# A feed-forward block with all 28 column tiles in pairs of seven products, and ten first products run ahead

## The chip, the cores and the metric

The kernel runs on one core of one Trainium2 chip. The metric is the device time of one execution in microseconds (us).

Short names: PE is the tensor engine (PEld its weight loads), DVE the vector engine, ACT the scalar engine, POOL the GpSimd engine, SP the engine that issues most of the loads.

## The reference

```python
B, S, D, F = 32, 32, 1024, 3584          # 1024 rows of x, bf16
def reference(x, w_gate, w_up, w_down):
    return (_gelu(x @ w_gate) * (x @ w_up)) @ w_down
```

## The kernel before

The hidden width of 3584 is 28 column tiles of 128. x is cut into two halves of 512 rows (`x0`, `x1`). Two column tiles, a left and a right one, together with the two halves of the rows and of the inner dimension, make a 2x2 block product. It needs 8 block products directly, and 7 in the Winograd form used here. A block product of one weight (gate or up) is four matmuls of 128x128 by 128x512, so for the two weights a pair costs 7 x 2 x 4 = 56 matmuls, where two tiles done directly cost 64.

Products 1 and 2 use plain bf16 operands. Products 3 to 7 use sums (and two plain operands) kept as fp32r: `S` holds the sums of x, `T` those of the weights.

Thirteen pairs cover 26 tiles. Tiles 0 and 1 are done directly. For four pairs product 1 runs ahead, at the start, when only `x0` is there: product 2 follows it into the same bank, which gives the left tile's first half of rows, and a copy of product 1 is kept for later. Such a pair is called short.

```python
LEFT = [2, 3] + list(range(4, 14)) + [14]
RIGHT = [26, 27] + list(range(16, 26)) + [15]
NP, EARLY = len(LEFT), 4
... (tiles 0 to 3 with x0: 64 matmuls, tiles 0 and 1 with x1: 32 matmuls)
for p in (2, 3):                                  # run ahead: products 1 and 2
    at = 25.8 + (p - 2) * 3.46
    g, u = 2 * p, 2 * p + 1
    for b, j, k0 in ((g, 0, 0), (u, 1, 0), (g, 0, 4), (u, 1, 4)):
        for k in range(k0, k0 + 4):
            mm(b, stat(p, j, k), x0[:, k, :], k == 0, k in (3, 7), add=k > 3)
        if k0 == 0:
            act(kept[p][:, j, :], bank(b), COPY, at + 0.9 * (j + 1))
    ...
sums_x(0, 21) ... sums_w(0, 4, 33.9)              # what the first pair needs
for p in range(NP):
    short, last = p < EARLY, p == NP - 1
    ...
    if short:
        for j in range(2):
            act(bank(B[j]), kept[p][:, j, :], COPY, at(0.1 + j * 0.1))
    else:
        for j in range(2):
            product(1, j, A[j], True)
            move(A[j], B[j], at(0.95 * (j + 1)))
    product(5, 0, E[0], True)
    ... (6, 7, 3 and 4; a full pair ends with product 2)
    sums_w(p + 1, 0, at(o + 1), "pool", [t4])     # T of the next pair: POOL, DVE, ACT
```

An `at` is only a sorting key: engines other than PE execute their instructions in that order, PE in the order of the program. Waits come from tracked reads and writes. After the pairs comes the down projection, 392 matmuls, which the change leaves alone but for the engine of its last copies.

## Time and profile before

| what | value | where it is read |
|---|---|---|
| time | 275.11 us (274.6 to 275.31) | three executions |
| span | 272.7 us, clock 1.00 | profile page |
| PE busy | 98% of the span | profile page |
| bf16 matmul to bf16 matmul | 0.216 us | starts of PE |
| fp32r matmul to fp32r matmul | 0.227 us | starts of PE |
| full pair, short pair | 12.56 us, 9.07 us | timelines of PE and DVE |

The head of the profile page of the kernel before: busy microseconds of each engine with its share of the span and its instructions, then busy tenths in 40 equal slices.

```profile
PE 268.1 (98%) x1186; PEld 188.1 (69%) x1200; DVE 189.2 (69%) x221; ACT 125.7 (46%) x195; POOL 45.4 (17%) x27
PE   8999999999999999999999999999999999999995
PEclk9999999999999999999999999999999999999999
PE 98%; issue 0%; DVE 0%
```

The last line is the chain of waits that ended last, by engine: followed back from the end it hardly leaves PE. The timeline of PE in the kernel before (start us, length us, what, count; a missing record here and there lowers a count by one):

```profile
4.61 28.16 PE L117 MATMUL ps<-arena 128*128 128x512 bf16 x126
32.42 36.66 PE L117 MATMUL ps<-S,T 128*128 128x512 f32 x160
...
92.54 3.40 PE L117 MATMUL ps<-arena 128*128 128x512 bf16 x15
95.59 9.44 PE L117 MATMUL ps<-S,T 128*128 128x512 f32 x40
105.10 3.40 PE L117 MATMUL ps<-arena 128*128 128x512 bf16 x15
...
182.24 24.12 PE L117 MATMUL ps<-arena,hT 128*128 128x512 bf16 x109
```

Up to 32.42 us PE works on bf16 products that need no sums. Then four short pairs follow in one piece (160 = 4 x 40 matmuls), then nine full pairs of 105.10 - 92.54 = 12.56 us each, and at 182.24 us the down projection starts.

### The profile page before, as it was taken

To read this page: it belongs to the slowest core of one execution; us is meant where nothing else is said; L and a number is where in the kernel's file an instruction comes from. 1 tells how busy PE (TensorE), PEld (TensorE's weight loads), DVE (VectorE), ACT (ScalarE), POOL (GpSimd) and SP (SyncE) were. 2 spreads that over 40 slices of the span, in tenths; PEclk is the share of its full clock that TensorE was granted. 3 is DMA by queue.
4 is the path that set the end of the run, shared out by engine and by line. 5 is a ranking of instruction groups with operands and counts; after the bars stand their busy time and mean duration, and the time that the engine had idled before them with its cause. 6 is when DMAs were issued, how large, how long until landed. Compare 5 with 4: busy or idle time off the path is not lost.

```text
span 272.7 us, 3266 instructions
## 1 busy us (share of the span) xinstructions
PE 268.1 (98%) x1186; PEld 188.1 (69%) x1200; DVE 189.2 (69%) x221; ACT 125.7 (46%) x195; POOL 45.4 (17%) x27
## 2 busy tenths in 40 slices
PE   8999999999999999999999999999999999999995
PEld 4444588888767686868676776664447888888884
DVE  1059978988583939374664739289962999999942
ACT  2344757566556474646455564521220112255561
POOL 1000032035326060524335160000000000000000
PEclk9999999999999999999999999999999999999999
DMA  7999412954700090047005000995011000001112
GB/s 184 270 207 300 117 39 60 281 202 124 186 0 0 21 286 2 0 129 179 1 4 154 0 2 0 302 350 159 0 38 38 2 0 0 1 2 58 38 58 77
DMA packets 44783, 26.42 MB, mean 97 GB/s; under 512 B 8416, under 2 KB 44768, under 8 KB 44768
## 3 DMA queue, kind: packets, MB, share of 16 engines
q1 hardware_dynamic: 42544, 24.25, 32.3%
q10 hardware_dynamic: 2224, 1.97, 2.8%
q8 instruction: 9, 0.15, 0.2%
q14 instruction: 6, 0.05, 0.1%
HBM read 22.28 MB, written 2.10 MB: 89 GB/s over the span
## 4 chain that ended last, share of the span: by engine, by line
PE 98%; issue 0%; DVE 0%
PE ps L117 98%; DVE arena L117 0%
## 5 line engine op out<-in xcount | busy, mean ns | idle before, releaser
L117 PE MATMUL ps<-S,T 128*128 128x512 f32 x520 | 122.0, 393 | 0.0
L117 PEld LDWEIGHTS ps<-S,T 128*128 128x128 f32 x520 | 97.7, 188 | 21.3
L117 ACT ACTIVATE tmp<-ps 128x512 f32<-128x512 f32 x64 | 38.1, 598 | 62.0 <-PE ps L117 62.0
L117 POOL TENSOR_TENSOR T<-arena 128x1024 fp32r<-128x1024 bf16 x21 | 44.7, 2149 | 117.1 <-PE ps L117 66.7
L117 PE MATMUL ps<-arena 128*128 128x512 bf16 x261 | 59.0, 379 | 0.8
L117 PE MATMUL ps<-T,S 128*128 128x512 f32 x224 | 51.3, 390 | 0.0
L117 ACT ACTIVATE ps<-ps 128x512 f32<-128x512 f32 x52 | 30.2, 583 | 42.0 <-PE ps L117 42.0
L117 DVE TENSOR_TENSOR hT<-tmp,ps 128x512 bf16<-128x512 f32 x56 | 37.2, 684 | 17.3 <-PE ps L117 14.9
L117 DVE TENSOR_TENSOR T<-arena,T 128x1024 fp32r<-128x1024 bf16 x40 | 48.4, 1217 | 0.1
L117 PEld LDWEIGHTS ps<-arena 128*128 128x128 bf16 x272 | 25.1, 98 | 33.4 <-issue 3.4
L117 PEld LDWEIGHTS ps<-T,S 128*128 128x128 f32 x224 | 42.1, 188 | 8.8
L117 DVE TENSOR_TENSOR tmp<-ps,tmp 128x512 f32<-128x512 f32 x26 | 18.0, 692 | 41.9 <-PE ps L117 41.9
L117 DVE TENSOR_TENSOR T<-arena 128x1024 fp32r<-128x1024 bf16 x19 | 22.7, 1218 | 7.4 <-PE ps L117 7.4
L117 PE MATMUL ps<-arena,hT 128*128 128x512 bf16 x109 | 24.0, 379 | 0.2
L117 DVE TENSOR_TENSOR ps<-ps,tmp 128x512 f32<-128x512 f32 x30 | 20.9, 695 | 2.8 <-PE ps L117 2.8
L117 PEld LDWEIGHTS ps<-arena,hT 128*128 128x128 bf16 x112 | 10.9, 98 | 13.2 <-issue 0.3
L117 ACT ACTIVATE tmp<-tmp 128x512 f32<-128x512 f32 x26 | 16.4, 632 | 4.2 <-DVE tmp L117 3.5
L117 DVE TENSOR_TENSOR S<-hT 128x1024 fp32r<-128x1024 bf16 x14 | 16.6, 1218 | 0.0
L117 ACT ACTIVATE T<-arena 128x1024 fp32r<-128x1024 bf16 x13 | 13.7, 1055 | 0.0
L117 PE MATMUL ps<-S 128*128 128x512 f32 x56 | 12.9, 389 | 0.0
L117 PEld LDWEIGHTS ps<-S 128*128 128x128 f32 x56 | 10.5, 188 | 2.2
L117 ACT ACTIVATE S<-arena 128x1024 fp32r<-128x1024 bf16 x9 | 9.4, 1057 | 4.3 <-PE ps L117 3.0
(25 smaller groups left out, 62.1 us busy)
## 6 DMA issues: line engine op xcount, KB each, us to landing
arena<-in_w_down_dram SPq DMA_DIRECT2D x4, 1792.0 KB, 10.5
arena<-in_w_gate_dram SPq DMA_DIRECT2D x11, 512.0 KB, 5.5
arena<-in_w_up_dram SPq DMA_DIRECT2D x11, 512.0 KB, 6.4
out_dram<-arena SPq DMA_DIRECT2D x12, 128.0 KB, 1.7
arena<-in_w_up_dram ACTq DMA_DIRECT2D x4, 128.0 KB, 4.5
arena<-in_w_gate_dram ACTq DMA_DIRECT2D x2, 256.0 KB, 5.0
arena<-in_w_up_dram ACTq DMA_DIRECT2D x2, 256.0 KB, 5.5
arena<-in_w_gate_dram SPq DMA_DIRECT2D x2, 256.0 KB, 6.3
```

Source lines behind the costliest of these rows:

```text
L117: ins = name(eng, *args, **kw) if callable(name) else getattr(eng, name)(*args, **kw)
```

## The change

Tiles 0 and 1 join the pairs: 14 pairs of tiles p and p + 14. The direct products of tiles 0 and 1 with the second half of x disappear, and PE would then run out of work before `x1` and its sums are ready. So products 1 and 2 of ten pairs instead of four run ahead. That needs the left weights of ten pairs early. There is no room for those of pairs 8 and 9, so they are put into half of the temporary buffer `tmp`, which the main loop overwrites, and are loaded a second time for the sums. The second pair of right weights takes the place of `x1` and is loaded once that has been read. The second half of x is now loaded after the weights of pairs 4 to 7. The first 64 matmuls now give eight copies of first products to keep instead of four; four of the eight are made by DVE, where all were made by ACT. The last output copies swap engines.

```diff
-        LEFT = [2, 3] + list(range(4, 14)) + [14]
-        RIGHT = [26, 27] + list(range(16, 26)) + [15]
-        NP, EARLY = len(LEFT), 4
+        NP, EARLY = 14, 10
+        kept = [piece(hT[:, m:m + 2, :]) for m in (14, 16, 18, 20, 22, 24, 26, 10, 12)] + [piece(o11[:, :, :])]
-        t0 = 33.0
+        t0 = 39.6
-        (tiles 0 and 1 with x1: 32 matmuls)
+        PLACE = [(None, 4096), (None, 0), (8192, 4096), (12288, 0), (20480, 24576), (8192, 12288), (20480, 24576)]
+        brief = tmp[:, 4:8, :] ...                    # pairs 8 and 9, while they run ahead
+        load_duo(2, 0, 10, None, 2, [begin_late])
+        load_duo(3, 0, 11, None, 2)
+        for k0 in range(0, DK, 2):
+            pr.add("sp", "dma_start_transpose", xT[1][:, k0:k0 + 2, :], xf[512:1024, ...], at=12, ...)
+        load_duo(4, 0, 13, brief)
+        load_duo(0, 1, 14)
-        for p in (2, 3):
-            at = 25.8 + (p - 2) * 3.46
+        for p in range(4, EARLY):
+            at = 18.9 + (p - 4) * 3.46
+            g = (0, 2, 4, 6, 2, 0)[p - 4]
+            for q, g, s in ((1, 2, 1), (3, 3, 1), (3, 4, 0), (3, 4, 1), (5, 5, 0), (7, 5, 1), (9, 6, 0), (9, 6, 1)):
+                if p == q:
+                    load_duo(g, s, t0)
             ... (cut: order of the first sums, names, the down projection's last copies)
```

More of the change, by code (lines that the diff above doesn't have):

```diff
@@ L161, in bass_standalone__geglu_ffn__sampling_kernel, with duo @@
         xT = [arena[:, a:a + 4096].rearrange("p (k n) -> p k n", n=512) for a in (16384, 0)]
-        raw_at = (20480, 8192)
-        raw = [arena[:, a:a + 8192].rearrange("p (s j k c) -> p s j k c", s=2, j=2, k=DK) for a in raw_at]
-        first = arena[:, raw_at[0]:raw_at[0] + 8192].rearrange("p (j k c) -> p j k c", j=2, k=DK)
-        near = arena[:, 4096:8192].rearrange("p (j k c) -> p j k c", j=2, k=DK)
+        first = arena[:, 20480:28672].rearrange("p (j k c) -> p j k c", j=2, k=DK)
+        def duo(a): return arena[:, a:a + 4096].rearrange("p (j k c) -> p j k c", j=2, k=DK)
         wd = [[arena[:, a:a + 7168].rearrange("p (k n) -> p k n", n=512) for a in row] for row in ((0, 7168), (14336, 21504))]
@@ L229, in bass_standalone__geglu_ffn__sampling_kernel, with piece @@
                 pr.add("dve", "tensor_copy", xT[0][:, k, i * 256:(i + 1) * 256], half)
-        LEFT = [2, 3] + list(range(4, 14)) + [14]
-        RIGHT = [26, 27] + list(range(16, 26)) + [15]
-        NP, EARLY = len(LEFT), 4
-        def left(p): return LEFT[p]
-        def right(p): return RIGHT[p]
-        kept = [hT[:, m:m + 2, :].rearrange("p t n -> p (t n)").bitcast(FP32).rearrange("p (j n) -> p j n", j=2)
-                for m in (10, 12, 22, 24)]
+        NP, EARLY = 14, 10
+        def piece(a): return a.rearrange("p t n -> p (t n)").bitcast(FP32).rearrange("p (j n) -> p j n", j=2)
+        kept = [piece(hT[:, m:m + 2, :]) for m in (14, 16, 18, 20, 22, 24, 26, 10, 12)] + [piece(o11[:, :, :])]
         SLOT = 0.9064
-        t0 = 33.0
+        t0 = 39.6
         T0 = []
@@ L257, in bass_standalone__geglu_ffn__sampling_kernel @@
             steps += [(m, j, k) for j in range(2) for k in range(DK - KO, DK)] + [(m, None, None)]
-        tile = lambda m: (m + 2) % 4
         for m, j, k in steps:
@@ L262, in bass_standalone__geglu_ffn__sampling_kernel @@
                 act(tmp[:, m, :], bank(2 * m), GELU, at)
-                tt(hT[:, tile(m), 0:512], tmp[:, m, :], bank(2 * m + 1), MUL, at)
+                tt(hT[:, m, 0:512], tmp[:, m, :], bank(2 * m + 1), MUL, at)
                 continue
-            op = mm(2 * m + j, first[:, j, k, tile(m) * P:(tile(m) + 1) * P], xT[0][:, k, :], k == 0, k in (3, DK - 1), add=k > 3)
-            if k == 3 and m < 2:
-                act(kept[m][:, j, :], bank(2 * m + j), COPY, 10.5)
+            op = mm(2 * m + j, first[:, j, k, m * P:(m + 1) * P], xT[0][:, k, :], k == 0, k in (3, DK - 1), add=k > 3)
+            if k == 3:
+                if m % 2 == 0:
+                    act(kept[m][:, j, :], bank(2 * m + j), COPY, 10.5)
+                else:
+                    pr.add("dve", "tensor_copy", kept[m][:, j, :], bank(2 * m + j), at=10.5)
             if (m, j) == (3, 1):
@@ L272, in bass_standalone__geglu_ffn__sampling_kernel, with load_duo @@
                 if k == 3:
-                    for k0 in range(0, DK, 2):
-                        load_x(1, k0, k0 + 2, [op])
-        steps = [(m, j, k) for m in range(2) for j in range(2) for k in range(KO)]
-        steps += [(m, j, k) for k in range(KO, DK - KO) for j in range(2) for m in range(2)]
-        for m in range(2):
-            steps += [(m, j, k) for j in range(2) for k in range(DK - KO, DK)] + [(m, None, None)]
-        for m, j, k in steps:
-            if j is None:
-                at = 25.0 + m * 0.87
-                act(tmp[:, m, :], bank(2 * m), GELU, at)
-                tt(hT[:, m, 512:1024], tmp[:, m, :], bank(2 * m + 1), MUL, at)
-                continue
-            mm(2 * m + j, first[:, j, k, m * P:(m + 1) * P], xT[1][:, k, :], k == 0, k == DK - 1)
-        def load_near(at):
-            for j in range(2):
-                dma("sp", near[:, j, :, :], w_r[j][:, :, right(0) * P:(right(1) + 1) * P], at, f"near{j}")
-        def load_pairs(gi, s, at, ks=slice(0, DK)):
-            for j in range(2):
-                m = (left, right)[s](2 * gi)
-                dma("sp", raw[gi % 2][:, s, j, ks, :], w_r[j][:, ks, m * P:(m + 2) * P], at, f"w{gi}_{j}{s}_{ks.start}")
-        load_near(10)
-        load_pairs(1, 0, 11, slice(0, 4))
-        load_pairs(1, 0, 11, slice(4, 8))
-        load_pairs(1, 1, 12)
+                    begin_late = op
+        PLACE = [(None, 4096), (None, 0), (8192, 4096), (12288, 0), (20480, 24576), (8192, 12288), (20480, 24576)]
+        brief = tmp[:, 4:8, :].rearrange("p t n -> p (t n)").bitcast(BF16).rearrange("p (j k c) -> p j k c", j=2, k=DK)
+        def load_duo(g, s, at, place=None, parts=1, after=()):
+            m, n = 2 * g + 14 * s, DK // parts
+            place = duo(PLACE[g][s]) if place is None else place
+            for k in range(0, DK, n):
+                for j in range(2):
+                    dma("sp", place[:, j, k:k + n, :], w_r[j][:, k:k + n, m * P:(m + 2) * P], at, f"w{g}{s}{j}{k}", after)
+                    after = ()
+        load_duo(2, 0, 10, None, 2, [begin_late])
+        load_duo(3, 0, 11, None, 2)
+        for k0 in range(0, DK, 2):
+            pr.add("sp", "dma_start_transpose", xT[1][:, k0:k0 + 2, :], xf[512:1024, k0 * P:(k0 + 2) * P], at=12, dma=f"x{k0}_1")
+        load_duo(4, 0, 13, brief)
+        load_duo(0, 1, 14)
         def load_wd(i, j, at):
@@ L307, in pair_w @@
         def pair_w(p, s, ks):
-            col = slice((p % 2) * P, (p % 2 + 1) * P)
-            if p < 2:
-                return first[:, :, ks, slice((p + 2) * P, (p + 3) * P)] if s == 0 else near[:, :, ks, col]
-            if p == NP - 1:
-                return raw[0][:, 0, :, ks, slice(s * P, (s + 1) * P)]
-            return raw[(p // 2) % 2][:, s, :, ks, col]
+            a = PLACE[p // 2][s]
+            if a is None:
+                return first[:, :, ks, p * P:(p + 1) * P]
+            return duo(a)[:, :, ks, (p % 2) * P:(p % 2 + 1) * P]
         def sx(s, k): return S[:, 4 * s + k:4 * s + k + 2, :]
@@ L327, in sums_x @@
                 elif s == 3:
-                    tt(sx(3, k), x0[:, k + 4:k + 6, :], sxf(1, k), SUB, at)
+                    tt(sx(3, k), x0[:, k + 4:k + 6, :], sxf(1, k), SUB, at + 1.5 * k)
                 else:
-                    act(sx(4, k), x1[:, k + 4:k + 6, :], COPY, at)
+                    act(sx(4, k), x1[:, k + 4:k + 6, :], COPY, at + 1.73 * k)
         def unit(p, u): return (5 * p + u) % 8
@@ L346, in sums_w, with stat @@
                 return tt(o, blk(1, 0), f(1), SUB, at, eng, after)
-        def stat(p, j, k): return pair_w(p, 0, slice(k, k + 1))[:, j, 0, :]
-        for p in (2, 3):
-            at = 25.8 + (p - 2) * 3.46
-            g, u = 2 * p, 2 * p + 1
+        def stat(p, j, k):
+            if p in (8, 9):
+                return brief[:, j, k, (p % 2) * P:(p % 2 + 1) * P]
+            return pair_w(p, 0, slice(k, k + 1))[:, j, 0, :]
+        for p in range(4, EARLY):
+            at = 18.9 + (p - 4) * 3.46
+            g = (0, 2, 4, 6, 2, 0)[p - 4]
+            u = g + 1
             for b, j, k0 in ((g, 0, 0), (u, 1, 0), (g, 0, 4), (u, 1, 4)):
@@ L357, in bass_standalone__geglu_ffn__sampling_kernel @@
                     act(kept[p][:, j, :], bank(b), COPY, at + 0.9 * (j + 1))
-            act(tmp[:, p, :], bank(g), GELU, at + 2.7)
-            tt(hT[:, left(p), 0:512], tmp[:, p, :], bank(u), MUL, at + 3.6)
-        sums_x(0, 21)
-        sums_x(1, 23.4)
-        sums_w(0, 0, 24.5)
-        sums_w(0, 1, 27)
-        sums_x(2, 28)
-        sums_w(0, 2, 29)
-        sums_x(3, 30.3)
-        sums_x(4, 22)
-        sums_w(0, 3, 28.6)
-        t4 = sums_w(0, 4, 33.9)
+            act(tmp[:, p % 4, :], bank(g), GELU, at + 2.7)
+            tt(hT[:, p, 0:512], tmp[:, p % 4, :], bank(u), MUL, at + 3.6)
+        sums_x(0, 27)
+        sums_x(1, 28)
+        sums_x(2, 30.5)
+        sums_w(0, 0, 33.5)
+        sums_w(0, 1, 34.5)
+        sums_w(0, 2, 36.5)
+        sums_x(3, 37.2)
+        sums_x(4, 28)
+        sums_w(0, 3, 36)
+        t4 = sums_w(0, 4, 40.5)
+        load_duo(1, 1, 34)
         B, C = (4, 5), (6, 7)
@@ L376, in bass_standalone__geglu_ffn__sampling_kernel @@
             A, E = ((0, 1), (2, 3)) if short or (p - EARLY) % 2 == 0 else ((2, 3), (0, 1))
-            if p % 2 == 0 and 2 <= p // 2 + 1 < (NP + 1) // 2:
-                load_pairs(p // 2 + 1, 0, t0)
-                if p < NP - 3:
-                    load_pairs(p // 2 + 1, 1, t0)
-            if p == 3:
+            for q, g, s in ((1, 2, 1), (3, 3, 1), (3, 4, 0), (3, 4, 1), (5, 5, 0), (7, 5, 1), (9, 6, 0), (9, 6, 1)):
+                if p == q:
+                    load_duo(g, s, t0)
+            if p == 7:
                 load_wd(0, 0, t0)
-            if last:
+            if p == 12:
                 load_wd(0, 1, t0)
-            ml, mr = left(p), right(p)
+            ml, mr = p, p + 14
             at = lambda s: t0 + s * SLOT
@@ L563, in done4 @@
         def done4(t, at):
-            if t % 2:
+            if t % 2 == 0:
                 pr.add("dve", "tensor_copy", late[:, 2, t, :], bank(PA[t]), at=at)
```

## The prediction

> **What bounds the kernel.** The tensor engine. The profile page gives PE 98% busy of a 272.7 us span, and the chain of waits that ended last is 98% PE, with pieces of "issue" of 0.05 to 0.07 us between; the granted clock is 1.00 in every slice. The Trainium skill ("Perfetto Trace Analysis", Identifying the Most-Contended Engine) warns that busy matmuls alone do not prove this, so I read rates from starts in the timeline of PE: bf16 products follow each other every 0.216 to 0.217 us (the first 128 from 4.61 to 32.42 us). A full pair takes 12.56 us (92.54 to 105.10), a short pair, whose first product was run ahead, 9.07 us (the same DVE step at 46.45, 55.52, 64.59). The waits view gives PE 0.8 us of idle in all, before the kernel's own work. So time follows the number and kind of matmuls, unless the change makes a gap.
>
> **Removed and added.** Before: 128 bf16 matmuls up front (tiles 0 and 1 done directly, 64 matmuls, first products of four pairs), then 4 short and 9 full pairs. After: 160 up front (first and second products of ten pairs), 10 short and 4 full pairs. The instruction order confirms 1184 matmuls become 1176: 48 fewer bf16, 40 more fp32r. From trace durations:
> - 32 more bf16 up front: 32 x 0.2173 = +6.95 us
> - 6 more short pairs: 6 x 9.07 = +54.42 us
> - 5 fewer full pairs: -62.80 us
> Sum -1.43 us, all on the critical path as PE is the chain. The last copy of an output tile goes from DVE (0.69 us) to ACT (0.60): perhaps -0.1 us more at the end.
>
> **Moved, expected free.** DVE does 8.5 us of work in each 9.07 us short pair (windows view: 8.9 of 10 us at 40:50 and 50:60) and made no PE gap there; ten such pairs instead of four repeat a steady state. Two loads of 1 MB are repeated, one of them at the start: the queue must now bring 5 MB behind the first x and weights instead of 4 MB. Packets of weights ran at about 285 KB per us until 30.2 us before, so about 33 us now. The risk lies here: the second half of x now comes after 2 MB of weights, so it lands near 28 instead of 21.2 us, and DVE then does eight sums of x (1.22 us each), three of weights and four products between 28 and 44 us. My hand schedule has the sums of the first pair ready 1 to 2.5 us before PE asks (first at 39.3 us). The weights of pair 4 must land by 18.4 us; I expect the first at 16.5 us.
>
> **Prediction.** 275.1 - 1.4 = 273.7 us; range 273.0 to 274.8. Faster by over 2%: 0.01; within 2%: 0.97; slower: 0.02.
>
> **What shows each step right or wrong.** Fp32r matmuls start near 39.3 us with no gap before; short pairs stay at 9.07 us through pair 9; PE waits stay near zero; the down projection begins near 180.8 us (before 182.24); after it nothing changes. If the second half of x comes late, PE has gaps between 39 and 46 us, released by DVE sums. If weights come late, PE weight loads wait for DMA at 18 to 33 us.
>
> **What would make it wrong.** A start-up stall by DMA order (up to 1 to 2 us, which would eat the gain); DVE falling behind over ten short pairs (its spare is only 0.5 us in each); weight loads for the later pairs arriving late because a buffer comes free only when the pair before it is done; copies of eight first products at 10.5 us, which have to clear a bank within 1.7 us.

## The result and the profile after

The first six executions of the changed kernel gave 273.31 us in the median, the fast ones from 272.91 to 273.66 us. One took 978.18 us, and it was the profiled one. It is treated apart at the end of this section. Run again (experiment 1) the changed kernel gave 273.55 us against 275.27 us, a ratio of 0.9941 with a 95% interval of 0.992 to 0.9961. A ratio here is the mean time of one kernel's fast runs over that of the other's of the same rounds, so it is not quite the ratio of the medians. The gain is real and well under 2%.

All readings of the changed kernel are from that second, fast profile. The head of its page, with the same lines as before, except that this trace has no record of the granted clock and so no PEclk line; that PE ran at full speed is read from its starts, which lie 0.216 and 0.227 us apart as before:

```profile
PE 266.3 (98%) x1182; PEld 190.6 (70%) x1192; DVE 203.1 (75%) x237; ACT 131.8 (49%) x210; POOL 37.1 (14%) x23
PE   8999999999999999999999999999999999999995
PE 98%; issue 0%; ACT 0%; DVE 0%
```

The timeline of PE in the changed kernel:

```profile
4.47 27.94 PE L117 MATMUL ps<-arena 128*128 128x512 bf16 x126 [0.34 <-DVE arena L117]
32.24 7.07 PE L117 MATMUL ps<-arena,tmp 128*128 128x512 bf16 x31
38.96 91.07 PE L117 MATMUL ps<-S,T 128*128 128x512 f32 x400
130.10 1.67 PE L117 MATMUL ps<-arena 128*128 128x512 bf16 x7
...
180.38 24.12 PE L117 MATMUL ps<-arena,hT 128*128 128x512 bf16 x109
```

The products of pairs 8 and 9, whose weights lie among the temporaries, are the second line. Ten short pairs (400 matmuls) run from 38.96 us without a gap; the down projection starts at 180.38 us. Between the two profiles the pair stage went from 182.24 - 32.42 = 149.82 us to 180.38 - 38.96 = 141.42 us, that is -8.40 us where the sum in the prediction says 54.42 - 62.80 = -8.38 us. The front went from 32.42 to 38.96 us, +6.54 us where the prediction says +6.95. The difference of 0.41 us is mostly the start-up, which varies from one execution to the next: counted from the event of the next paragraph the front grew by 6.92 us. After the pairs the two differ by -0.12 us, most of it the last copy.

**A yardstick free of the start-up.** ACT's first GELU of a product waits for the 50th of the first 64 matmuls. Its start ranges from 15.46 to 17.05 us in nine profiles, although those kernels issue the same PE work up to there. In the kernel before and in the changed one:

```profile
15.84 0.60 ACT L117 ACTIVATE tmp<-ps 128x512 f32<-128x512 f32 x1 [3.33 <-PE ps L117]
15.46 0.60 ACT L117 ACTIVATE tmp<-ps 128x512 f32<-128x512 f32 x1 [3.33 <-PE ps L117]
```

Two things make up the spread of 1.6 us, which is as much as the whole gain. One is the clock: in two of the starts (eight ahead, x first) matmuls still follow each other every 0.427 us, double the usual 0.216, until 6.3 and 6.5 us. The Trainium skill, "TensorE: Matmul & The Clock Gate", Part 1, says that PE starts at half clock, that the warm-up window runs freely, and that its cost varies from run to run. The traces agree: the first matmuls lie 0.427 us apart in all nine, and the last at half clock comes between about 3.4 and 6.5 us. The other is the first loads: with nine ahead PE was at full clock by then but lost 1.1 us waiting for x, and with eight ahead 0.6 us waiting for up weights. So in the table below the last column subtracts the whole start-up: span minus the start of the first GELU.

| kernel | median us | ratio to before, 95% | span - first GELU, us | against the changed kernel |
|---|---|---|---|---|
| before | 275.27 | 1 | 272.74 - 15.84 = 256.90 | +1.60 |
| changed | 273.55 | 0.992 to 0.9961 | 270.76 - 15.46 = 255.30 | 0 |
| loads twice | 273.59 | 0.992 to 0.9954 | 271.13 - 15.87 = 255.26 | -0.04 |
| sum on DVE | 273.07 | 0.9901 to 0.9956 | 271.08 - 15.81 = 255.27 | -0.03 |
| eight matmuls more | 275.17 | 0.9973 to 1.0004 | 273.39 - 16.36 = 257.03 | +1.73 |
| nine ahead | 274.98 | 0.9955 to 0.9998 | 273.63 - 16.72 = 256.91 | +1.61 |
| x later | 275.46 | 0.9981 to 1.0014 | 273.16 - 16.27 = 256.89 | +1.59 |
| x first | 277.62 | 1.0063 to 1.0124 | 274.54 - 16.71 = 257.83 | +2.53 |
| eight ahead | 278.86 | 1.0101 to 1.0141 | 277.33 - 17.05 = 260.28 | +4.98 |

The medians and ratios come from three sets of rounds on three chips, in which the kernel before had medians of 275.27, 275.40 and 275.23 us; each ratio is to the kernel before of the same rounds. The last two columns are of one execution each. The three kernels with no extra PE work or wait agree there within 0.04 us, while their medians spread over 0.5 us.

**The slow execution.** Its page has no line of the granted clock and its clock is given as 1.0; the fast profile of the changed kernel lacks that line too. The timeline of PE shows what happened:

```profile
35.38 40.54 PE L117 MATMUL ps<-arena 128*128 128x512 bf16 x49 [0.52 <-issue]
```

With one missing record these are 50 matmuls in 76.44 - 35.38 = 41.06 us, 0.82 us each against 0.216, from the start to the end. PE ran at about a quarter of its speed; nothing else was slow (the DVE sums took 1.22 us as always). The same kernel did not show it in its eleven other executions, and none of the variants did. It says nothing about the change, and it is left out of all comparisons.

### The profile page after: what moved, and what is told of

It is laid out like the page before. It is cut to its first block, busy times and chain, and to the rows that moved or that the text cites. A ratio compares the mean times of both kernels' runs of the same rounds, so it can differ in the third digit from the quotient of the medians.

```text
span 976.1 us, 3280 instructions
## 1 busy us (share of the span) xinstructions
PE 966.8 (99%) x1182; PEld 436.0 (45%) x1192; DVE 208.5 (21%) x237; ACT 134.8 (14%) x210; POOL 36.6 (4%) x23
## 3 DMA queue, kind: packets, MB, share of 16 engines
HBM read 23.33 MB, written 2.10 MB: 26 GB/s over the span
## 4 chain that ended last, share of the span: by engine, by line
PE 99%; issue 1%; ACT 0%
PE ps L117 99%; ACT arena L117 0%
## 5 line engine op out<-in xcount | busy, mean ns | idle before, releaser
L117 PE MATMUL ps<-S,T 128*128 128x512 f32 x560 | 465.4, 1102 | 0.0
L117 PEld LDWEIGHTS ps<-S,T 128*128 128x128 f32 x560 | 240.2, 429 | 221.0 <-issue 212.7
L117 PE MATMUL ps<-T,S 128*128 128x512 f32 x224 | 185.2, 1098 | 0.0
L117 PE MATMUL ps<-arena 128*128 128x512 bf16 x186 | 155.2, 1105 | 3.4 <-issue 3.4
L117 PEld LDWEIGHTS ps<-T,S 128*128 128x128 f32 x224 | 96.0, 429 | 88.1 <-issue 88.1
L117 PEld LDWEIGHTS ps<-arena 128*128 128x128 bf16 x192 | 41.4, 221 | 113.9 <-issue 108.7
L117 PE MATMUL ps<-arena,hT 128*128 128x512 bf16 x109 | 90.2, 1106 | 1.9 <-issue 1.9
L117 PEld LDWEIGHTS ps<-arena,hT 128*128 128x128 bf16 x112 | 24.5, 221 | 67.1 <-issue 66.5
L117 PE MATMUL ps<-S 128*128 128x512 f32 x56 | 46.3, 1092 | 0.0
L117 PE MATMUL ps<-arena,tmp 128*128 128x512 bf16 x31 | 26.1, 1100 | 0.5 <-issue 0.5
```

Of the source, the lines that this page charges most:

```text
L117: ins = name(eng, *args, **kw) if callable(name) else getattr(eng, name)(*args, **kw)
```

## The experiments

### 1. The changed kernel again

No edit, for a fast profile.

> The changed kernel unaltered, because its profiled execution fell into a state of 976 us. Theory A (fewer matmuls, all on the PE chain): ratio 0.995, about 273.3 to 273.8 us; fp32r matmuls start near 39.3 us without a gap; short pairs at 9.07 us throughout; the down projection starts near 180.8 us. Rival B (the start-up stalls and the gain is larger elsewhere): a PE gap of over 0.3 us between 18 and 46 us, and the pairs faster than 9.07 or 12.56 us. If the 976 us execution belongs to the kernel it should come again in some of the runs; if it belongs to that chip or moment it should not.

Measured: 273.55 us, ratio 0.9941. Fp32r work starts at 38.96 us, with no gap, and the down projection at 180.38 us. The pairs keep their 9.07 us (DVE's same step at 53.00 and 62.07 us) and 12.56 us (153.49 to 166.05). The slow execution did not come again. Theory A holds.

### 2. Eight matmuls more

The last pair's product 1 is issued twice; the second overwrites the first.

```diff
                 for j in range(2):
+                    if last:
+                        product(1, j, A[j], True)
                     product(1, j, A[j], True)
```

> The changed kernel with the eight bf16 matmuls of product 1 of the last pair issued twice (the second overwrites the first): 1184 matmuls, as many as the kernel before. Theory A (each matmul on the chain is worth its whole slot): +1.73 us, ratio to the kernel before 0.999 to 1.001. Rival G (the gain comes from elsewhere, PE has room): ratio stays 0.994.

Measured: 275.17 us, ratio 0.9988 (0.9973 to 1.0004), result correct. By the yardstick it is +1.73 us, which is 8 x 0.216. The timeline of PE around the start of the last pair, in the changed kernel and then in this one (8 matmuls and 1.73 us more):

```profile
166.05 3.40 PE L117 MATMUL ps<-arena 128*128 128x512 bf16 x15
166.95 5.13 PE L117 MATMUL ps<-arena 128*128 128x512 bf16 x23
```

With as many matmuls as before, the kernel is as slow as before. So the gain is PE's matmul count, and each matmul is worth its full slot.

### 3. Eight and nine pairs ahead

The first attempt, with ten replaced by eight or nine:

```diff
-        NP, EARLY = 14, 10
+        NP, EARLY = 14, 8          # or 9
-        t0 = 39.6
+        t0 = 32.7                  # or 36.15
-            if p in (8, 9):
+            if 8 <= p < EARLY:
             ... (keys of the first sums moved ahead of the first pair; with 8, no load into tmp)
```

> All 28 tiles in 14 pairs, but only eight first products run ahead, so no weights among the temporaries and 1176 matmuls as in the changed kernel. Theory A (the two more pairs ahead buy no matmul, they only give PE 7 us of work until the sums of the second half of x are ready): PE must start fp32r work at 32.4 us, the sums for product 5 are ready at about 36 us and those for product 3 later, so a PE gap of 3 to 5 us and 276.5 to 278.5 us. Rival C (running ahead is not needed, only the fourteenth pair counts): same time as the changed kernel, within 0.3 us. Rival D (running ahead is itself the gain, fewer switches between bf16 and fp32r): slower by 0.1 to 0.2 us without any gap.

> As early8 with nine pairs ahead: PE reaches fp32r work at about 35.9 us. Theory A with my hand schedule (sums for product 5 ready at about 36.8, for product 3 at about 43): a PE gap of 0.5 to 1.5 us, 274.0 to 275.0 us. If the start-up has more slack than I think: no gap and the time of the changed kernel, within 0.2 us.

Both gave a wrong result (relative error 0.446) and 287.52 and 284.31 us. Pair 9 now does its product 2 in the main loop and still reads its left weights there, but the program had already issued the load that overwrites them. The tracked reads then waited for the wrong weights to arrive: in the trace with nine ahead PE stood idle for 7.72 us at pair 9, waiting for a weight load. The times say nothing about the theories. The mended kernels issue that load one pair later:

```diff
-            ... (9, 6, 0), (9, 6, 1)):
+            ... (9, 6, 1), (10, 6, 0)):
```

> early8 again, mended: there the load of the last pairs' weights was placed ahead of the reads of pair 9, so its result was wrong and it waited. All 28 tiles in 14 pairs, eight ahead, 1176 matmuls. Theory A (the two more pairs ahead buy no matmul, they give PE 7 us of work until the sums are ready): PE reaches fp32r work at about 32.1 us; in the trace of the changed kernel DVE starts the sums of x at 26.1 us and needs some 9 us for those ahead of product 5, so a PE gap of 3 to 4 us there and 276 to 277.5 us. Rival C (running ahead is not needed, only the fourteenth pair counts): the changed kernel's 273.5 us within 0.4 us. Rival D (running ahead itself is the gain through fewer switches): slower by 0.1 to 0.2 us, without a gap.

> early9 again, mended likewise: nine pairs ahead. The trace of the changed kernel shows the sums done 1.8 us (second half of the sum for product 3) to 2.7 us (first weight sum) before PE asks. PE now asks 3.45 us earlier, and DVE has one product (0.6 us) less to make. Theory A: a PE gap of 0.3 to 1.5 us, 273.8 to 275 us. Rival C: no gap.

Measured, both correct: 278.86 us with eight ahead and 274.98 us with nine. The two timelines of PE at the start of the pairs, eight ahead first (the bracket is the idle time before and what ended it):

```profile
37.01 74.43 PE L117 MATMUL ps<-S,T 128*128 128x512 f32 x320 [3.01 <-DVE T L117]
```

```profile
37.51 82.83 PE L117 MATMUL ps<-S,T 128*128 128x512 f32 x360 [0.39 <-DVE T L117]
```

PE waits for DVE's sums of the weights, as theory A has it; rivals C (no need to run ahead) and D (a gain by fewer switches) fall, because both kernels have 1176 matmuls and are slower than the changed kernel by 4.98 and 1.61 us by the yardstick.

With eight ahead the loss is larger than the 3 to 4 us expected, although the gap is of the expected size. The windows view of that kernel (us, then busy time of each engine with its instructions, granted clock, DMA share, GB/s) shows the rest:

```profile
30.00:35.00 5.00, 4.00 (x19) 1.46 (x17) 5.00 (x6) 4.10 (x8) 0.00 (x0) 1.00 0.29 71
35.00:40.00 5.00, 2.99 (x7) 2.41 (x8) 4.97 (x6) 1.92 (x3) 0.00 (x0) 0.70 0.75 205
40.00:45.00 5.00, 5.00 (x22) 4.10 (x22) 4.07 (x5) 3.01 (x5) 2.16 (x1) 0.96 0.02 4
```

DVE is full in the first two windows, and after the gap the granted clock falls to 0.70 on average over five microseconds. PE's starts then lie 0.427 us apart until about 40.5 us. Summing what each interval has over 0.227, the slow matmuls cost 1.7 us and the gap 3.2 us, together 4.9 of the 4.98. The Trainium skill, "TensorE: Matmul & The Clock Gate", gives one idle window of about 3.4 us as what brings the half clock back. Here a gap of 3.0 us in the profile's count did (3.2 us if a matmul is taken to hold PE for 0.216 us), and the windows view shows how it lies:

```profile
33.62:37.03 3.41, 0.40 (x3) 0.02 (x1) 3.38 (x5) 2.70 (x5) 0.00 (x0) 1.00 0.12 31
37.04:40.44 3.40, 3.40 (x8) 2.72 (x9) 3.40 (x4) 0.60 (x1) 0.00 (x0) 0.50 1.00 277
```

The clock record of this trace gives full clock from 6.32 to 37.04 us (30.72 us, nine times 3.413) and half clock for the next 3.413 us. In the other traces with such a record the stretches at full clock are whole multiples too (266.24 and 269.65 us, 78 and 79 times 3.413). So in these traces the clock changes on a grid of 3.413 us, and the gap, from 33.8 to 37.0 us, filled nearly the whole of one step of it. All four executions of this kernel have a mean clock of 0.993 or 0.994.

With nine ahead the loss is in small pieces: starts of PE further apart by about 1.0 us in sum from 36.7 to 38.8 us, and by 0.5 us from 49.6 to 51.5 us, a pair later.

### 4. The second half of x later, and first

"Later" puts its load behind the weights in the temporaries; "first" ahead of the weights of pairs 4 to 7, as in the kernel before.

```diff
-            pr.add("sp", "dma_start_transpose", xT[1][...], ..., at=12, ...)
+            pr.add("sp", "dma_start_transpose", xT[1][...], ..., at=13.5, ...)      # later
+            pr.add("sp", "dma_start_transpose", xT[1][...], ..., at=9, ..., after=[begin_late] if k0 == 0 else ())   # first
```

> The changed kernel with the second half of x loaded after the weights among the temporaries instead of before them: 1 MB, 3.5 us, later. Theory A with the slack read from the trace (DVE waits 0.84 us for weights in that stretch, the tightest sum is 1.8 us early): PE gap of 0.3 to 1.2 us near 43 us, 273.8 to 274.8 us. Rival F (start-up has several us to spare): no change within 0.3 us.

> The changed kernel with the second half of x loaded before the weights of pairs 4 to 7, the order that the kernel before had. Theory A with landings read from the trace: 1 MB of x takes about 5 us of the queue, so the weights of pair 4, which PE asks for at about 18 us, land 3 to 5 us later than in the changed kernel, where they were just in time: a PE gap of 2 to 4 us near 18 us by weight loads that wait for DMA, perhaps 1 to 2 us more because an idle PE runs on at half clock (as in early8b), 275.5 to 279 us. Rival F (start-up has several us to spare): no change within 0.3 us.

Measured: 275.46 us with x later, +1.59 us by the yardstick: more than the 0.3 to 1.2 us expected of the wait. The prediction of the place was off as well. Lines of the waits view of this kernel from 30 to 56 us (who waited for whom: us in total, times, longest):

```profile
DVE S L117 <- DMA arena<-in_x_dram: 3.2, 1, 3.2
ACT ps L117 <- DVE hT L117: 2.0, 1, 2.0
ACT S L117 <- DMA arena<-in_x_dram: 1.6, 1, 1.6
PE ps L117 <- ACT hT L117: 0.8, 1, 0.8
DVE T L117 <- POOL T L117: 0.5, 1, 0.5
PE ps L117 <- ACT ps L117: 0.2, 1, 0.2
```

PE never waited for a sum in the first pair. It waited for two other things. First, ACT executes in order: its copy of x for the sums stood in the queue, waited 1.6 us for x, and held up the copies of products 1 that free PE's banks; PE lost 0.95 us at 31.1 us. Second, DVE was late by then, its last sum of pair 0 releases POOL's first sum of pair 1 (2.16 us), DVE waits for that, and the product that frees the bank for the copy of pair 1's kept product comes late; PE lost 0.6 us from 52.5 to 54.5 us. My hand schedule looked at the direct users of the sums only.

With x first the time is 277.62 us. The timeline of PE:

```profile
22.07 14.14 PE L117 MATMUL ps<-arena 128*128 128x512 bf16 x64 [2.38 <-DMA arena<-in_w_gate_dram]
```

PE waits 2.38 us for the gate weights of pair 4, as theory A says, and +2.53 us by the yardstick is this wait alone (2.54 us from the starts). The clock did not fall after this gap in the profiled execution, which is the fastest of the four (276.61; the others 277.44 to 277.9). Its mean clock is 1.000; that of the other three is 0.993 or 0.994, as with eight ahead, where the trace shows 3.41 us at half clock. So they most likely lost about 1 us more to half clock after the same gap, but they were not profiled. That the same gap can go both ways would fit the grid: in the profiled execution full clock begins at 6.70 us, and four steps of 3.413 us later, at 20.35 us, a boundary cuts the gap from 19.5 to 22.1 us in two. This was not tested.

Rival F, that the start-up has several microseconds to spare, falls on both sides: the order of loads in the change is needed.

### 5. Every later weight load twice

```diff
                 if p == q:
                     load_duo(g, s, t0)
+                    load_duo(g, s, t0)
```

> The changed kernel with every weight load of the pair stage issued twice to the same place: 8 MB more from memory, eight times what the change added. Theory A (loads off the chain cost nothing): same time as the changed kernel within 0.3 us. Rival E (a repeated load costs PE or DVE time through contention): at least 1 us more, with longer DVE or matmul durations between 50 and 150 us.

Measured: 273.59 us, against 273.55 us for the changed kernel in the same rounds, and -0.04 us by the yardstick. 8 MB more of loads cost nothing that can be seen, so neither does the 1 MB that the change repeats.

### 6. One more sum on DVE in each short pair

```diff
-                sums_w(p + 1, 0, at(o + 1), "pool", [t4])
+                sums_w(p + 1, 0, at(o + 0.3), "dve") if p + 1 < EARLY else sums_w(p + 1, 0, at(o + 1), "pool", [t4])
```

> The changed kernel with the first weight sum of short pairs 1 to 9 on DVE (one 1.22 us instruction, 1.14 us from start to start) instead of POOL. Reading 1, that of the prediction (8.5 us busy in 9.07, 0.5 us spare): DVE is over-full by 0.65 us in each of eight pairs, so after some slack PE waits, +3 to +5 us. Reading 2, from gaps in the timeline of DVE (busy 7.9 of 9 us, durations overlap): 1.1 us spare, so it just fits, no more than +0.6 us.

Measured: 273.07 us, -0.03 us by the yardstick. No PE gap appeared. One window of about a pair in the changed kernel and then in this one (columns as in the windows view above):

```profile
57.00:66.00 9.00, 9.00 (x42) 7.44 (x41) 7.90 (x11) 5.80 (x11) 2.16 (x1) 1.00 0.00 0
```

```profile
57.00:66.00 9.00, 9.00 (x41) 7.48 (x40) 8.85 (x12) 5.91 (x10) 0.00 (x0) 1.00 0.00 0
```

DVE goes from 7.90 to 8.85 us of 9 and POOL from 2.16 to 0, and PE does not notice. Reading 2 holds: DVE had 1.1 us to spare in each short pair, not 0.5. The prediction added up durations, and these overlap: an instruction that lasts 1.22 us is followed by the next after 1.14 us. This is no faster version either, because DVE was not the limit.

## Why the prediction was right

- **What bounds it.** Right. PE works through its matmuls without gaps; eight more of them cost 1.73 us (experiment 2), and more loads or DVE work cost nothing that can be seen (5 and 6).
- **The sum of -1.43 us.** Right. By the yardstick the gain is 1.60 us. The pair stage changed by -8.40 us (said: -8.38). The front's change was 0.41 us smaller than said, mostly through start-up losses, which belong to the execution and not to the change; counted from the first GELU it is +6.92 us (said: +6.95). The last copy is 0.60 us instead of 0.69, as said. The program repeats one load of 1 MB (23.33 MB read from memory instead of 22.28), not two as the prediction says. Most of the gain is the fourteenth pair, 64 bf16 matmuls replaced by 16 bf16 and 40 fp32r. Running ahead moves work and by itself saves next to nothing: 9.07 + 3.475 us of a short pair, with its two products ahead, against 12.56 us.
- **The loads land in time.** Right for the change as it is: PE shows no wait for the weights of pair 4 or for sums. The second half of x came earlier than the prediction's 28 us: DVE began its sums at 26.14 us. Experiment 4 shows how near it was. One step the other way in the load order costs 2.5 us, one step this way 1.6 us, as much as the whole gain.
- **DVE's spare time of 0.5 us.** Wrong in size, without effect on the time: it is 1.1 us (experiment 6). The prediction summed overlapping durations.
- **Where a late x would be felt.** Not quite: it named DVE's sums between 39 and 46 us. With x later, PE waited at 31 us behind ACT's queue and at 52 us behind DVE, POOL and ACT one pair on (experiment 4).
- **What a gap costs.** Too small: it allowed 1 to 2 us for a stall, the gap alone. A gap of 3.0 us also cost 1.7 us at half clock (experiment 3), and one of 2.4 us probably about 1 us in three executions of four (experiment 4).

## What to carry to other kernels

When one engine is busy without gaps, count its instructions by kind, multiply by start-to-start intervals from the trace, and the gain of a change that removes a few of them is known to a few tenths of a microsecond, provided the change opens no gap. Work run ahead is then bought for its timing and not for its count, and it is worth the gap it fills: here two fewer pairs ahead cost 5 us, a gap of 3.2 us and 1.7 us of slow matmuls after it (with sums scheduled by hand; another order was not tried). To compare profiles finer than the start-up varies, subtract the time of a common early event; and when asking what a late load will hold up, follow every in-order queue in which its reader stands.

## What the Trainium skill lacked or had wrong

- "TensorE: Matmul & The Clock Gate", Part 1, gives about 3.4 us of idle before PE falls to half clock; its table of advice says about 3 us. Here a gap of 3.0 us did it (matmuls 0.427 us apart for the next 3.5 us, 1.7 us lost). One of 2.4 us did not in the profiled execution, but the mean clock of 0.993 or 0.994 in the other three executions of that kernel suggests that it did there. So the length of a gap alone may not decide it.
- The same page reports a clock seen stuck at a quarter for over 50 us. One execution here ran a whole 976 us with matmuls 0.82 us apart instead of 0.216, without a clock record and with the clock given as 1.0. It did not recur, and whether it is the same state is not shown.
- No page gives a start-to-start interval for fp32r matmuls with 512 columns: 0.227 us here, against 0.216 for bf16 (the page's 215.7 ns for bf16 agrees).
- "Perfetto Trace Analysis", Identifying the Most-Contended Engine, takes the occupancy of the vector engine as a fair measure, and does not say how overlapping records are to be counted. Here it matters: DVE's durations sum to about 8.5 us per short pair, merged they are 7.9 us of 9, since a 1.22 us instruction is followed after 1.14 us.
